# The first expert of the first pair of blocks is summed without gates and multiplied later; the flag of the general path is read four supersteps on

## The chip, the cores and the metric

The kernel runs on one core of one Trainium2 chip. The metric is the device time of one execution in microseconds (us). The engines are TensorE (PE; its weight loads are listed as PEld), VectorE (DVE), ScalarE (ACT), GpSimd (POOL) and SyncE (SP), which here only issues transfers.

## The reference, cut to what matters

A gated linear attention over 4 x 768 tokens, a squared-ReLU layer (384 to 2048 to 384), and then a mixture of eight experts, in which each of the 3072 tokens goes through every expert and the gates P weight the sums:

```python
logits = x @ w_gate
P = np.exp(logits - logits.max())
for _ in range(8):
    P /= P.sum(1, keepdims=True) + 1e-09
    P /= P.sum(0, keepdims=True) + 1e-09
    P *= N / E
out = np.zeros((N, D), dtype=np.float32)
for e in range(E):
    h = np.maximum(x @ w1[e], 0.0)
    ye = h @ w2[e]
    out += P[:, e:e + 1] * ye
```

P needs the logits of all tokens and eight rounds of sums over rows and columns (the Sinkhorn iterations). The expert sums `ye` need no gates until they are weighted.

## The kernel before

Two stages follow one another. The first computes attention and the squared-ReLU layer and writes x2, the input of the experts, to DRAM; it ends at about 594 us. The second is the mixture. It works through three pairs of blocks of 512 tokens; for each pair, through the eight experts; for each expert, through four steps of 256 hidden units. Every matmul of an fp32 product is done three times, on high and low parts.

A **step** runs eight products (`product`, L678; 33 matmuls of 512 columns) named `p1`, `p2`, `p6`, `p5`, `p3`, `p7`, `p22`, `p4`, in this order on PE. They share banks of PSUM, so DVE and ACT have to take sums out between them: ACT copies `s` (L696), DVE forms `t` (`part`, L700) and four sums `v` (`whole`, L705; `whole b` is the first). `p22` writes the bank that `part` reads. ACT makes the high part of the hidden values (L713), DVE the low part (L718). The weights of a step come through `rawa` and `rawc`: POOL forms sums (L650 to L652), ACT high parts (L663), DVE low parts, here called residuals (L667).

Two steps make a **superstep** `q`, of which there are 48, two to an expert and pair. It ends with six tiles `o` (`second`, L729; 12 matmuls each, 2 token blocks `t` by 3 output blocks `m`), which have two PSUM banks. DVE evicts each (`weigh`, L744): it multiplies the tile by the gates `pb` of its tokens, which a transfer has broadcast over the partitions (`ldp`, L736), into the accumulator `acc` for an expert's first superstep of a pair and otherwise into a scratch tile `sc`, which POOL adds to `acc` (`gather`, L749). After the last expert SP stores `acc`.

The gates are made while the first superstep runs: per iteration DVE's row part (L960 to L964), a column sum on PE (`csum`, L967, two passes) and DVE's column part (L971 to L974); then PE transposes P (`pt`, L845), ACT copies it (`pts`, L850), SP stores it (`ptd`, L853) and loads it as `pb`.

A **flag** tells whether the decays of the attention were in range. DVE and POOL reduce it (`in_range`, L883 to L886) after superstep 10, and every engine reads it into a register (L887); at the end a branch on it runs a general path, or not.

The order of all of this on each engine is planned ahead. `Plan` holds steps with an engine, a duration, a due time and needs. `order` plays them through a model of engines that take the step with the earliest due time among the ready ones, and `emit` writes the program in that order. A step that is given other needs can so move on every engine. On the chip each engine takes its instructions in the order written.

```python
add(("skr", it), "dve", 1.7, d, lambda: sk.rows(P), [done], lag=0.8)
add(("skt", it), "pe", 0.1, d, csum, [("skr", it)])
add(("skc", it), "dve", 0.9, d, sk_cols, [("skt", it)])
```

Of the kernel before, what the change touches and what calls it, by code (L numbers as in the profile page):

```python
# [9 lines left out]
F32 = mybir.dt.float32  # L10
# [26 lines left out]
TB = 512  # L37
# [113 lines left out]
def body(tc, fkq, v, wm, wa, wc, gate, seqs, out):  # L151
# [585 lines left out]

    def weigh(q, t, m):
        p, e, s = pair_of(q)
        if e == 0 and s == 0:  # L740
            dst = acc[p, t, m] = pools["acc"].tile([128, TB], F32, name=f"acc{t}{m}")
        else:
            dst = sc[q, t, m] = pools["v"].tile([128, TB], F32, tag="sc", name="sc", bufs=2)
        dve.tensor_tensor(out=dst, in0=ob[q, t, m], in1=pbt[p, e][:, t * TB:(t + 1) * TB], op=ALU.mult)  # L744

    def gather(q, t, m):
        p, e, s = pair_of(q)
        if e or s:
            pool.tensor_tensor(out=acc[p, t, m], in0=acc[p, t, m], in1=sc[q, t, m], op=ALU.add)  # L749
        if e == NE - 1 and s == NST // 2 - 1:  # L750
            o = (2 * p + t) * TB
            sp.dma_start(out=out[m, :, o:o + TB], in_=acc[p, t, m])
# [29 lines left out]
    for g in range(NSTEP):  # L782
        p, r = divmod(g, NE * NST)
        u = at(t_step(g))
        uw = u - 6.0
        plan.load(("ldwa", g), 393, uw - 1.5, lambda g=g: ldwa(g), slot_of["wa", g])
        plan.load(("ldwc", g), 393, uw - 1.4, lambda g=g: ldwc(g), slot_of["wc", g])
        add(("wsum", g), "pool", 1.7, uw, lambda g=g: w_sum(g), [("ldwa", g)])
        for k in "abc":

            n = 3 * g + "abc".index(k) - NWP
            if n >= 0:
                free = ("p4", n // 3) if n % 3 < 2 else ("o", n // 6, 1, 2)
            else:
                free = ("e2", n1 - NF + n + NWP)
            add(("w2hi", g, k), "act", 0.6 if k == "b" else 0.82, uw, lambda g=g, k=k: w2_hi(g, k),
                [("ldwc", g) if k == "c" else ("ldwa", g), ("wsum", g) if k == "b" else None, free,
                 ("w2hi", g, "abc"["abc".index(k) - 1]) if k != "a" else ("w2hi", g - 1, "c") if g else None])
            add(("w2lo", g, k), "dve", 0.7 if k == "b" else 0.96, uw, lambda g=g, k=k: w2_lo(g, k), [("w2hi", g, k)])
        needs = {"p1": [("w2lo", g, "a"), ("w2lo", g, "b"), ("take", g - 1, 3)], "p2": [("whole", g - 1, "b")], "p6": [("take", g, 1)],  # L800
                 "p5": [("whole", g - 1, "c"), "right"], "p3": [("whole", g - 1, "d")], "p7": [("take", g, 2)], "p22": [("part", g)],
                 "p4": [("whole", g - 1, "e")]}
        if r == 0:
            needs["p1"] += [("xlo", p, n) for n in range(3)]
        for n, name in enumerate(PROD):
            if g == 0:
                needs[name] = [d for d in needs[name] if not (isinstance(d, tuple) and d[1] == -1)]
            add((name, g), "pe", 0.68 * len(PROD[name][1]), u + 0.1 * n, lambda g=g, name=name: product(g, name), needs[name] + [last_pe])
            last_pe = (name, g)
        for n, name in ((1, "p1"), (2, "p6"), (3, "p7")):  # L810
            old = {1: "b", 2: "d", 3: "e"}[n]
            add(("take", g, n), "act", 0.6, u + 0.3, lambda g=g, n=n: take(g, n), [(name, g), ("whole", g - 1, old) if g else None])
        add(("part", g), "dve", 0.69, u + 0.3, lambda g=g: part(g), [("p5", g), ("take", g, 2), "right", ("whole", g - 1, "d") if g else None])
        order = "bdce"
        for k, src, other in (("b", "p2", ("take", g, 1)), ("d", "p3", ("part", g)), ("c", "p22", ("take", g, 3)), ("e", "p4", ("take", g, 3))):
            add(("whole", g, k), "dve", 0.69, u + 0.5, lambda g=g, k=k: whole(g, k), [(src, g), other, "right"] + [("whole", g, order[order.index(k) - 1]) if k != "b" else ("whole", g - 1, "e") if g else None]
                + [("hlo", g, "b") if k == "e" else ("hlo", g - 1, order[order.index(k) + 1]) if g else None])
            t, f = TF[k]
            add(("hhi", g, k), "act", 0.61, u + 0.6, lambda g=g, k=k: hid_hi(g, k),
                [("whole", g, k), ("o", g // 2 - 1, t, 2) if g >= 2 else None])  # L820
            add(("hlo", g, k), "dve", 0.69, u + 0.6, lambda g=g, k=k: hid_lo(g, k), [("hhi", g, k)])
        if g % 2 == 0:
            continue
        q = g // 2
        p, e, s = pair_of(q)
        if s == 0:
            n = p * NE + e
            old = pair_of(q - 2 * (NST // 2)) if n >= 2 else None
            plan.load(("ldp", p, e), 524, u - 3.0, lambda p=p, e=e: ldp(p, e), ["P", "right", ("ev", q - NST // 2 - 1, 1, 2) if n >= 2 else None])
        for t in range(2):  # L830
            for m in range(KD):
                d = at((q + 1) * T_SUP - T_E2) + 0.9 * (KD * t + m)
                i = KD * t + m
                free = ("ev", q, (i - 2) // KD, (i - 2) % KD) if i >= 2 else (("ev", q - 1, (i + 4) // KD, (i + 4) % KD) if q else None)
                add(("o", q, t, m), "pe", 2.72, d, lambda q=q, t=t, m=m: second(q, t, m),
                    [("hlo", 2 * q + f // 2, k) for f in range(4) for k in TF if TF[k] == (t, f % 2)] + [("w2lo", 2 * q, "c"), ("w2lo", 2 * q + 1, "c"), free, last_pe])
                last_pe = ("o", q, t, m)
                add(("ev", q, t, m), "dve", 0.69, d + 0.9, lambda q=q, t=t, m=m: weigh(q, t, m), [("o", q, t, m), ("ldp", p, e), ("ac", q - 1, t, m) if q else None,
                     ("ac", q, (i - 2) // KD, (i - 2) % KD) if i >= 2 else ("ac", q - 1, (i + 4) // KD, (i + 4) % KD) if q else None])
                add(("ac", q, t, m), "pool", 1.35, d + 0.9, lambda q=q, t=t, m=m: gather(q, t, m), [("ev", q, t, m)])  # L840

    def gates_turn(n):
        tmp["pt"] = ps_m.tile([24, 4, 128], F32, tag="m", name="pt")
# [38 lines left out]
    def in_range():  # L882
        dve.tensor_reduce(out=mx, in_=minf, axis=AX.XY, op=ALU.min)  # L883
        dve.tensor_scalar(out=mx, in0=mx, scalar1=MIN_DECAY, scalar2=None, op0=ALU.is_lt)
        pool.partition_all_reduce(gmx, mx, 128, bass.bass_isa.ReduceOp.max)
        dve.tensor_copy(out=flag, in_=gmx)  # L886
        general.append(nc.values_load(flag[0:1, 0:1], min_val=0, max_val=1))  # L887

    add("range", "dve", 1.0, n1 + 200, in_range, ["P", ("o", 10, 1, 2)])

    with tc.manual_schedule():
        plan.emit(keep_warm)
# [277 lines left out]
```

## Time and profile before

| | us |
|---|---|
| median of 3 runs | 2159.89 (2159.45 to 2163.94) |
| the profiled execution | 2158.78, of which its span 2157.1 |
| PE busy | 2083.4, 97% of the span |
| DVE, ACT, POOL busy | 1323.9, 886.1, 646.8 |

The profile is one execution. Its timeline gives start, length, engine, line, operation and tile of each group of neighbouring instructions, and in brackets how long the engine was idle before it and what ended that. Instructions of one engine overlap by some hundredths of a microsecond in it. [...]

### The profile page before, as it was taken

What the parts mean: (1) busy time and instruction counts of PE and PEld (TensorE: products, weight loads), DVE (VectorE), ACT (ScalarE), POOL (GpSimd) and SP (SyncE); (2) the same over time, 40 slices, a digit from 0 to 9 for tenths busy, and PEclk for the clock granted to TensorE, in tenths of its full rate; (3) what the DMA queues carried; (4) which work ended last, traced back from release to release, by engine and by line L of the source; (5) the groups of instructions that cost most, each with busy time, mean ns of one, the idle gap of its engine ahead of it and who ended that gap; (6) DMA issues with size and microseconds to landing.
All of it is one profiled execution on the core that took longest, in us unless ns stands there. A gap on an engine that the chain in (4) does not pass through costs nothing.

```text
span 2157.1 us, 27848 instructions
## 1 busy us (share of the span) xinstructions
PE 2083.4 (97%) x10686; PEld 1765.9 (82%) x10686; DVE 1323.9 (61%) x2016; ACT 886.1 (41%) x1505; POOL 646.8 (30%) x642
## 2 busy tenths in 40 slices
PE   7889999999959999999999999999999999999998
PEld 5779899999947888887887888888887888888886
DVE  8973444332465676675677666667668666766663
ACT  4754444444623343343344334334434433433341
POOL 4531101100102334333423333333333233343332
PEclk9899999999979999999999999999999999999999
DMA  7331222110201111121123121112113111211210
GB/s 265 126 126 64 76 82 73 54 44 7 85 34 53 59 60 62 56 69 47 52 73 108 54 69 54 62 52 69 55 54 127 55 55 58 65 57 54 69 45 31
DMA packets 55114, 148.76 MB, mean 69 GB/s; under 512 B 6332, under 2 KB 15548, under 8 KB 54972
## 3 DMA queue, kind: packets, MB, share of 16 engines
q1 hardware_dynamic: 54972, 146.90, 20.7%
q8 instruction: 85, 1.39, 0.3%
q14 instruction: 57, 0.47, 0.1%
HBM read 135.28 MB, written 9.54 MB: 67 GB/s over the span
## 4 chain that ended last, share of the span: by engine, by line
PE 89%; DVE 6%; DMA 1%; issue 1%; POOL 1%; ACT 1%; SPq 0%; POOLq 0%; DVEq 0%; ACTq 0%
PE o L729 35%; PE e L678 33%; PE a L525 8%; PE e L499 8%; PE y L383 1%; PE y L386 1%; PE pp L344 1%; DVE cv_t L923 1%; PE lg L540 1%; DVE cv_t L915 1%; DVE lo L515 1%; DVE sg L318 1%; DVE cv_t L919 0%; POOL acc L749 0%; PE ds L366 0%
## 5 line engine op out<-in xcount | busy, mean ns | idle before, releaser
L729 PE MATMUL o<-h,w 128*128 128x512 f32 x3456 | 794.6, 390 | 7.4 <-DVE acc L744 7.4
L729 PEld LDWEIGHTS o<-h,w 128*128 128x128 f32 x3456 | 650.4, 188 | 143.7 <-DVE acc L744 7.9
L678 PE MATMUL e<-x,w 128*128 128x512 f32 x3168 | 732.8, 391 | 9.7 <-DVE flag L886 4.6
L678 PEld LDWEIGHTS e<-x,w 128*128 128x128 f32 x3168 | 597.7, 189 | 136.2 <-ACT s L696 5.6
L749 POOL TENSOR_TENSOR acc<-acc,sc 128x512 f32<-128x512 f32 x270 | 350.0, 1303 | 574.0 <-DVE sc L744 565.7
L696 ACT COPY s<-e 128x512 f32<-128x512 f32 x288 | 169.1, 587 | 849.6 <-PE e L678 844.8
L744 DVE TENSOR_TENSOR sc<-o,pb 128x512 f32<-128x512 f32 x270 | 186.3, 690 | 384.6 <-PE o L729 349.4
L718 DVE SCALAR_TENSOR_TENSOR h<-v,h 128x512 fp32r<-128x512 f32 x384 | 276.7, 740 | 1.7 <-ACT h L713 1.3
L713 ACT ACTIVATE h<-v 128x512 fp32r<-128x512 f32 x384 | 242.5, 632 | 41.8 <-DVE v L705 41.8
L650 POOL TENSOR_TENSOR rawa<-rawa 128x256 f32<-128x256 f32 x96 | 83.4, 869 | 550.2 <-DMA rawa<-in_wa_dram 375.8
L705 DVE TENSOR_TENSOR v<-e,s 128x512 f32<-128x512 f32 x288 | 198.2, 688 | 75.2 <-ACT w L663 58.1
L499 PE MATMUL e<-x,w 128*128 128x384 f32 x1152 | 228.0, 341 | 10.9 <-DVE w L283 7.4
L499 PEld LDWEIGHTS e<-x,w 128*128 128x128 f32 x1152 | 199.8, 189 | 17.7 <-DVE w L283 8.8
L515 DVE TENSOR_TENSOR lo<-g,hi 128x384 fp32r<-128x384 f32 x128 | 85.0, 666 | 206.3 <-ACT hi L511 206.3
L525 PE MATMUL a<-hi,w 128*128 128x384 f32 x768 | 199.5, 341 | 0.0
L667 DVE TENSOR_TENSOR w<-rawa,w 128x768 fp32r<-128x768 f32 x192 | 158.0, 824 | 7.4 <-ACT w L663 7.4
L663 ACT CAST w<-rawa 128x768 fp32r<-128x768 f32 x192 | 135.2, 729 | 27.9 <-POOL rawa L652 9.3
L525 PE MATMUL a<-lo,w 128*128 128x384 f32 x384 | 131.0, 341 | 11.0 <-DVE lo L515 10.9
L525 PEld LDWEIGHTS a<-hi,w 128*128 128x128 f32 x768 | 139.9, 191 | 1.5 <-issue 0.3
L504 ACT ACTIVATE g<-e 128x384 f32<-128x384 f32 x128 | 62.9, 491 | 178.0 <-PE e L499 157.3
L328 POOL TENSOR_TENSOR kq<-kq,sg 128x512 f32<-128x512 f32 x24 | 30.9, 1287 | 289.4 <-DVE sg L318 172.1
L667 DVE TENSOR_TENSOR w<-rawc,w 128x768 fp32r<-128x768 f32 x96 | 91.6, 954 | 0.3 <-ACT w L663 0.2
(99 smaller groups left out, 1300.8 us busy)
## 6 DMA issues: line engine op xcount, KB each, us to landing
rawa<-in_wa_dram SPq DMA_DIRECT2D x96, 384.0 KB, 3.0
rawc<-in_wc_dram SPq DMA_DIRECT2D x96, 384.0 KB, 3.4
raw<-in_wm_dram SPq DMA_DIRECT2D x16, 768.0 KB, 6.1
pb<-ptd SPq DMA_DIRECT2D x24, 512.0 KB, 3.6
fraw<-in_fkq_dram SPq DMA_DIRECT2D x23, 512.0 KB, 3.8
kq<-in_fkq_dram SPq DMA_DIRECT2D x23, 512.0 KB, 4.4
vt<-in_v_dram SPq DMA_DIRECT2D x24, 192.0 KB, 4.9
x2d<-x2t SPq DMA_DIRECT2D x8, 576.0 KB, 2.8
```

The source lines that it names most:

```text
L499: pe.matmul(ps, w[:, wl, k * 128:(k + 1) * 128], xx[:, xl, k, :], start=n == 0, stop=n == 3 * KD - 1)
L525: pe.matmul(acc1[j][m], w[:, wl, D + m * 128:D + (m + 1) * 128], g, start=f == 0 and n == 0, stop=f == NF - 1 and n == 2)
L663: act.copy(out=W2[g, k][:, 0, 0:n], in_=src)
L667: dve.tensor_tensor(out=W2[g, k][:, 1, 0:n], in0=src, in1=W2[g, k][:, 0, 0:n].bitcast(F32), op=ALU.subtract)
L678: pe.matmul(ps, w[a], x[b], start=start and n == 0, stop=stop and n == 2, skip_group_check=True)
L696: act.copy(out=snap[g, n], in_=bank[g, "a"])
L705: dve.tensor_tensor(out=vs[g, k], in0=bank[g, k], in1=other, op=ALU.add)
L713: act.activation(out=hs[g // 2, t, f][:, 0], in_=vs[g, k], func=ACTF.Relu)
L718: dve.scalar_tensor_tensor(out=h[:, 1], in0=vs[g, k], scalar=0.0, in1=h[:, 0].bitcast(F32), op0=ALU.max, op1=ALU.subtract)
L729: pe.matmul(ob[q, t, m], w[:, a, c:c + 128], h[:, b], start=f == 0 and n == 0, stop=f == 3 and n == 2)
L744: dve.tensor_tensor(out=dst, in0=ob[q, t, m], in1=pbt[p, e][:, t * TB:(t + 1) * TB], op=ALU.mult)
L749: pool.tensor_tensor(out=acc[p, t, m], in0=acc[p, t, m], in1=sc[q, t, m], op=ALU.add)
```

## The change

For expert 0 of the first pair (supersteps 0 and 1) `weigh` uses no gates: superstep 0's tiles are copied into `acc`, superstep 1's are added to it by DVE. After that POOL multiplies each `acc` by the gates once (`scale0`), in place, and superstep 2's additions to it wait for this. The evictions of these two supersteps no longer need `ldp`. In the very last superstep DVE, not POOL, does the additions of `gather`. The reduction of the flag stays after superstep 10, its read (`choose`) waits for superstep 14.

```diff
     def weigh(q, t, m):
         p, e, s = pair_of(q)
+        if p == 0 and e == 0:
+
+            if s == 0:
+                acc[p, t, m] = pools["acc"].tile([128, TB], F32, name=f"acc{t}{m}")
+                dve.tensor_copy(out=acc[p, t, m], in_=ob[q, t, m])
+            else:
+                dve.tensor_tensor(out=acc[p, t, m], in0=ob[q, t, m], in1=acc[p, t, m], op=ALU.add)
+            return
...
+    def scale0(t, m):
+        pool.tensor_tensor(out=acc[0, t, m], in0=acc[0, t, m], in1=pbt[0, 0][:, t * TB:(t + 1) * TB], op=ALU.mult)
+
     def gather(q, t, m):
         p, e, s = pair_of(q)
+        eng = dve if q == NSUP - 1 else pool
         if e or s:
-            pool.tensor_tensor(out=acc[p, t, m], in0=acc[p, t, m], in1=sc[q, t, m], op=ALU.add)
+            eng.tensor_tensor(out=acc[p, t, m], in0=acc[p, t, m], in1=sc[q, t, m], op=ALU.add)
...
-                add(("ev", q, t, m), "dve", 0.69, d + 0.9, lambda q=q, t=t, m=m: weigh(q, t, m), [("o", q, t, m), ("ldp", p, e), ("ac", q - 1, t, m) if q else None,
+                add(("ev", q, t, m), "dve", 0.69, d + 0.9, lambda q=q, t=t, m=m: weigh(q, t, m), [("o", q, t, m), ("ldp", p, e) if p or e else None, ("ac", q - 1, t, m) if q else None,
...
-                add(("ac", q, t, m), "pool", 1.35, d + 0.9, lambda q=q, t=t, m=m: gather(q, t, m), [("ev", q, t, m)])
+                if p == 0 and e == 0:
+                    add(("ac", q, t, m), "none", 0, d + 0.9, lambda: None, [("ev", q, t, m)])
+                    if s == NST // 2 - 1:
+                        add(("sc0", t, m), "pool", 1.35, d + 1.5, lambda t=t, m=m: scale0(t, m), [("ac", q, t, m), ("ldp", 0, 0)])
+                else:
+                    last = q == NSUP - 1
+                    add(("ac", q, t, m), "dve" if last else "pool", 0.69 if last else 1.35, d + 0.9, lambda q=q, t=t, m=m: gather(q, t, m),
+                        [("ev", q, t, m), ("sc0", t, m) if p == 0 and e == 1 and s == 0 else None])
...
+
+    def choose():
         general.append(nc.values_load(flag[0:1, 0:1], min_val=0, max_val=1))
 
     add("range", "dve", 1.0, n1 + 200, in_range, ["P", ("o", 10, 1, 2)])
+    add("choose", "dve", 0.1, n1 + 230, choose, ["range", ("o", 14, 1, 2)])
```

How the change moves instructions is seen at three places. In these rows a number behind a name (`e_5852`) tells one buffer from another, `x7` is a count, and brackets name the engines or transfers that are waited for.

The first place is PE at the gates. Before, the seven remaining column sums and the transpositions stand between the second and the third `o` tile of superstep 0:

```order
L729 MATMUL o<-h,w_5072 128x512 x6
L729 MATMUL o<-h,w_5260 128x512 x6
L967 MATMUL csum<-sk_cs,sk_ones 128x8 [waits DVE_49] x7
L845 MATMUL pt<-shift,P 24x128 [waits DVE_49]
L845 MATMUL pt<-shift,P 24x128 x3
L845 MATMUL pt<-shift,P 24x128 [waits Activation_49]
L845 MATMUL pt<-shift,P 24x128 x3
L729 MATMUL o<-h,w_5072 128x512 [waits DVE_49]
```

Now the sums are spread over the tiles of superstep 0 and the two steps of superstep 1; this is the end of the second step, up to the first `o` of superstep 1:

```order
L678 MATMUL e_5828<-x_5132,w_5583 128x512 x2
L989 MATMUL csum<-sk_cs,sk_ones 128x8 [waits DVE_49] x2
L678 MATMUL e_5852<-x_5131,w_5406 128x512 [waits DVE_49]
L678 MATMUL e_5852<-x_5131,w_5406 128x512 x2
L678 MATMUL e_5906<-x_5131,w_5583 128x512 x3
L678 MATMUL e_5906<-x_5131,w_5406 128x512 x3
L864 MATMUL pt<-shift,P 24x128 [waits DVE_49]
L864 MATMUL pt<-shift,P 24x128 x3
L864 MATMUL pt<-shift,P 24x128 [waits Activation_49]
L864 MATMUL pt<-shift,P 24x128 x3
L729 MATMUL o<-h,w_5354 128x512 x6
```

Here the last two sums are neighbours, `e_5852` with three matmuls is `p22`, the two rows of `e_5906` are `p4`, and the transpositions stand ahead of superstep 1's tiles instead of superstep 0's third.

The second place is DVE at the gates. Before, the iterations follow one another there, and the first evictions come behind the last column part:

```order
L964 TENSOR_REDUCE sk_cs<-P 128x8 [waits DVE_49]
L971 TENSOR_SCALAR sk_cs<-csum 128x8 [waits PE_49]
L972 RECIPROCAL sk_cs<-sk_cs 128x8 [waits DVE_49]
L973 TENSOR_SCALAR sk_cs<-sk_cs 128x8 [waits DVE_49]
L974 TENSOR_TENSOR P<-P,sk_cs 128x192 [waits DVE_49]
L744 TENSOR_TENSOR acc_5749<-o,pb 128x512 [waits DMAHW4_49]
L744 TENSOR_TENSOR acc_5751<-o,pb 128x512
```

Now steps of superstep 1 stand between the iterations; these rows are what lies on DVE behind the column sum that is the last but one:

```order
L718 SCALAR_TENSOR_TENSOR h<-v,h 128x512 [waits Activation_49] x2
L993 TENSOR_SCALAR sk_cs<-csum 128x8 [waits PE_49]
L994 RECIPROCAL sk_cs<-sk_cs 128x8 [waits DVE_49]
L995 TENSOR_SCALAR sk_cs<-sk_cs 128x8 [waits DVE_49]
L996 TENSOR_TENSOR P<-P,sk_cs 128x192 [waits DVE_49]
L982 TENSOR_REDUCE sk_rs<-P 128x24 [waits DVE_49]
L983 TENSOR_SCALAR sk_rs<-sk_rs 128x24 [waits DVE_49]
L984 RECIPROCAL sk_rs<-sk_rs 128x24 [waits DVE_49]
L985 TENSOR_TENSOR P<-P,sk_rs 128x192 [waits DVE_49]
L986 TENSOR_REDUCE sk_cs<-P 128x8 [waits DVE_49]
L718 SCALAR_TENSOR_TENSOR h<-v,h 128x512 [waits Activation_49]
L700 TENSOR_TENSOR t<-e_5852,s_5860 128x512
```

The last column sum on PE takes the `sk_cs` of the third row from below, and the `p22` behind it takes the bank that the last row (`part`) reads.

The third place is DVE at the flag, before:

```order
L883 TENSOR_REDUCE mx<-minf 128x1
L884 TENSOR_SCALAR mx<-mx 128x1 [waits DVE_49]
L886 CAST flag<-gmx 128x1 [waits Pool_49]
L887 TENSOR_LOAD flag [waits DVE_49]
L705 TENSOR_TENSOR v<-e_8426,s_8433 128x512 [waits PE_49,Activation_49]
L667 TENSOR_TENSOR w_8454<-rawa,w_8454 128x768 [waits DMAHW1_49,Activation_49]
L700 TENSOR_TENSOR t<-e_8463,s_8467 128x512 [waits PE_49,Activation_49]
```

and now:

```order
L902 TENSOR_REDUCE mx<-minf 128x1
L903 TENSOR_SCALAR mx<-mx 128x1 [waits DVE_49]
L905 CAST flag<-gmx 128x1 [waits Pool_49]
L705 TENSOR_TENSOR v<-e_8420,s_8427 128x512 [waits PE_49,Activation_49]
L667 TENSOR_TENSOR w_8434<-rawa,w_8434 128x768 [waits DMAHW1_49,Activation_49]
L700 TENSOR_TENSOR t<-e_8443,s_8447 128x512 [waits PE_49,Activation_49]
```

The read (`TENSOR_LOAD`) has gone from there, on PE, ACT, POOL and SP as well, to the beginning of superstep 15; the cast, which waits for POOL, is still ahead of `whole b`, a residual and `part`.

## Rows read from the trace of the kernel before

**Rows 1.** The page: the chain by engine, and the group of evictions (busy, mean ns)

```profile
PE 89%; DVE 6%; DMA 1%; issue 1%; POOL 1%; ACT 1%; SPq 0%; POOLq 0%; DVEq 0%; ACTq 0%
...
L744 DVE TENSOR_TENSOR sc<-o,pb 128x512 f32<-128x512 f32 x270 | 186.3, 690 | 384.6 <-PE o L729 349.4
```

**Rows 2.** PE's waits: in total (us), times, longest

```profile
PE csum L967 <- DVE sk_cs L964: 18.1, 6, 3.1
```

**Rows 3.** The timeline of PE around the gates (start, length, engine, line)

```profile
616.61 0.28 PE L967 MATMUL csum<-sk_cs,sk_ones 128*128 128x8 f32 x2
620.04 0.39 PE L967 MATMUL csum<-sk_cs,sk_ones 128*128 128x8 f32 x2 [3.15 <-DVE sk_cs L964]
...
641.16 1.03 PE L845 MATMUL pt<-shift,P 128*24 128x128 f32 x4 [0.66 <-ACT pts L850]
649.60 13.67 PE L729 MATMUL o<-h,w 128*128 128x512 f32 x48 [7.41 <-DVE acc L744]
663.11 15.12 PE L678 MATMUL e<-x,w 128*128 128x512 f32 x66
678.07 12.18 PE L729 MATMUL o<-h,w 128*128 128x512 f32 x53
```

**Rows 4.** The chain that ended last, in order of time: start, us, what

```profile
642.83 1.99 DMA ptd<-pts
644.88 3.95 DMA pb<-ptd
...
678.23 16.32 PE o L729 x72
```

**Rows 5.** The timeline at the flag, DVE and PE

```profile
975.91 2.20 PE L678 MATMUL e<-x,w 128*128 128x512 f32 x9
...
982.01 0.15 DVE L886 CAST flag<-gmx 128x1 int32<-128x1 f32 x1 [4.89 <-POOL gmx L885]
...
982.76 14.86 PE L678 MATMUL e<-x,w 128*128 128x512 f32 x57 [4.65 <-DVE flag L886]
983.28 0.69 DVE L705 TENSOR_TENSOR v<-e,s 128x512 f32<-128x512 f32 x1 [1.11 <-issue]
983.89 0.95 DVE L667 TENSOR_TENSOR w<-rawa,w 128x768 fp32r<-128x768 f32 x1
```

**Rows 6.** The timeline of DVE: one Sinkhorn iteration, ends of its two parts

```profile
635.89 0.35 DVE L960 TENSOR_REDUCE sk_rs<-P 128x24 f32<-128x192 f32 x1
...
637.22 0.50 DVE L964 TENSOR_REDUCE sk_cs<-P 128x8 f32<-128x192 f32 x1
...
638.40 0.17 DVE L971 TENSOR_SCALAR sk_cs<-csum 128x8 f32<-128x8 f32 x1 [0.69 <-PE csum L967]
...
639.05 0.36 DVE L974 TENSOR_TENSOR P<-P,sk_cs 128x192 f32<-128x192 f32 x1
```

**Rows 7.** Windows of PE: us, PE busy (count), granted clock, DMA share, GB/s

```profile
620.00:622.00 2.00, 0.39 (x2) 0.71 0.05 18
...
654.00:656.00 2.00, 2.00 (x8) 0.76 0.00 0
...
982.00:983.00 1.00, 0.24 (x1) 0.82 0.00 0
...
986.00:987.00 1.00, 1.00 (x6) 0.97 0.00 0
...
1140.00:1142.00 2.00, 1.40 (x7) 1.00 0.02 8
1142.00:1144.00 2.00, 0.69 (x3) 1.00 0.26 97
```

**Rows 8.** The timeline of DVE and POOL: a residual at 615, and the tail

```profile
615.66 0.68 DVE L667 TENSOR_TENSOR w<-rawa,w 128x512 fp32r<-128x512 f32 x1
...
2147.53 0.69 DVE L744 TENSOR_TENSOR sc<-o,pb 128x512 f32<-128x512 f32 x1 [2.03 <-PEq L894]
2148.30 1.26 POOL L749 TENSOR_TENSOR acc<-acc,sc 128x512 f32<-128x512 f32 x1 [1.43 <-DVE sc L744]
```

More of the change, by code (lines that the diff above doesn't have):

```diff
@@ L828, in body @@
             old = pair_of(q - 2 * (NST // 2)) if n >= 2 else None
-            plan.load(("ldp", p, e), 524, u - 3.0, lambda p=p, e=e: ldp(p, e), ["P", "right", ("ev", q - NST // 2 - 1, 1, 2) if n >= 2 else None])
+            plan.load(("ldp", p, e), 524, u - 3.0, lambda p=p, e=e: ldp(p, e), ["P", "right", ("ev", q - NST // 2 - 1, 1, 2) if n >= 2 else None, ("sc0", 1, 2) if n == 2 else None])
         for t in range(2):
```

## The prediction

> **What bounds the kernel now.** I read the chain that ended last first: 89% of it is TensorE (PE) [rows 1]. So only stretches in which PE stands or runs at its lower clock are worth anything. PE's waits name the largest, the column sums of the gates [rows 2]; PE's own timeline shows what lies around it [rows 3]. Between 616.61, where 24 `o` matmuls are through, and 649.60 us PE runs seven column sums and the transpositions of the gates, nothing else. In order, that is: the Sinkhorn iterations on VectorE (DVE), two transpositions, the store of the gates, the broadcast load `pb`, and the first eviction that multiplies by `pb`; PE has only two `o` banks, and both are full. A second stretch is the read of the flag, a third the tail after the last matmul.
>
> **Prices.** A 512-column matmul at full clock: 16.32 / 72 = 0.227 us [rows 4], so an `o` tile of twelve is 2.72 us. A 128x512 DVE step takes 0.61 us to the start of the next (983.28 to 983.89), a 768-column one 0.95 - 0.08 = 0.87 [rows 5]. A Sinkhorn iteration on DVE: its rows 635.89 to 637.72, 1.83 us; its columns 638.40 to 639.41, 1.01; together 2.84 [rows 6].
>
> **Part 1: the gates leave the path of the first expert.** Removed: the first `o` evictions no longer wait for `pb`. Six multiplications become copies and six become additions on DVE. No row shows a 128x512 copy out of PSUM on DVE; I take the 0.69 us of the multiplication that it replaces [rows 1], and between 0.35 and 0.75 nothing changes below, since the copies wait for PE. POOL loses six additions of `q` = 1 and gets six multiplications of the same shape: nothing.
>
> The new order interleaves the seven remaining column sums with the matmuls, so both engines have to be walked. Nothing differs up to 616.61. From there PE has four `o` tiles (10.88), the nine matmuls `p1` and `p2` of the next step (2.04) and two column sums (0.15 each, an estimate from the 0.28 of two passes [rows 3]): it is through with `p2` at 629.9. DVE keeps up that far: six copies, two weight residuals and two iterations are 6 x 0.61 + 1.5 + 2 x 2.84 = 10.8 of these 13.3 us, and each copy comes right behind its tile.
>
> From 629.9 DVE is the bound. Up to the step `part` (L700) of the second step, for which PE's `p22` waits, its order holds four iterations (11.36) and ten 128x512 steps (6.1): 17.5 us, so `part` ends at 647.4. PE has less to do and stands four times: about 0.7 us before the first `p22`, 0.3 before the sixth of the seven sums, and then 3.9 us between two neighbouring column sums, because a whole iteration and two DVE steps lie between them; and 0.9 more for `part`. After 647.4 PE has nine matmuls, the two groups of transpositions (2 x 1.03 and 0.66 between them at the lower clock [rows 3]), and then the `o` tiles of the second superstep, which started at 678.07 before.
>
> The clock decides the last step. After PE stopped at 616.9, with a column sum at 620.04, the granted clock left 1.0 at about 620.8 (0.71 over 620 to 622), and it was back at about 655.0, after 5.4 us of matmuls; at the flag it fell at 982.6 after a stop at 978.1 and was back at 986.06, after 3.3 us [rows 7]. The stop from 642.5 to 647.4, with one column sum in it, is like these. So I take half clock (1.2 GHz) for the nine matmuls and the transpositions: 647.4 + 4.1 + 2.7 = 654.2. Gain: 678.07 - 654.2 = **23.9 us**. If the clock holds, nine matmuls take 2.04, and ScalarE's chain (L713, then `pts`) makes the second transposition end at about 652: gain 26. If every one of the four iterations shows a hop of 0.4 to PE and back, the gain is 22.3. PE's own work, with no wait and no fall, would end at about 644.5: 33.6 is the most that is there.
>
> What is late next: gates are ready at about 654, `pb` lands 2 + 4 us later [rows 4] at about 660, and its first reader is now POOL (`scale0`), ahead of the weight sums of step 6. These reach PE at about 701. Four multiplications of 1.3 us have some 30 us of slack. The loads of step 5 stand between `ptd` and `pb` in SP's queue and are needed at about 678; they land by 660.
>
> **Part 2: the flag.** Only the read moves. DVE still runs the cast of the flag, which waits for POOL's reduction, until 982.16 [rows 5]: DVE stays blocked from 977.1, with whatever stands behind it. Before, PE stood behind its own read: superstep 11's 66 matmuls took from 975.91 to 997.46 (982.76 + 14.86, less the 0.16 by which neighbouring groups overlap in this view: 663.11 + 15.12 against 678.07 [rows 3]), 21.55 us against 66 x 0.227 = 14.96: 6.6 lost, 4.65 standing and the rest at the lower clock. Now PE goes on after `p2` until `p22`, 24 matmuls after 975.91, at 981.35. `p22` needs `part`, and DVE reaches it after the cast, `whole b` and a weight residual: 982.16 + 0.61 + 0.87 + 0.69 = 984.3. PE stands 3.0 us instead. Gain **3.6 us** if the clock holds, 3.6 - 1.65 = 1.95 if it falls (half of the 3.3 us). A stop of 1.91 (0.60 and 1.31 in two windows) left it at 1.00 [rows 7]; those of 3.15 and more did not. 3.0 lies nearer to the second, but the fall after 616.9 came only in the following stop; I take no fall.
>
> The read itself stands four supersteps on, when the flag is long there. From the end of the cast to PE's next matmul were 0.60 us [rows 5], so its price is 0 to 0.6; DVE and ScalarE have it in idle time (DVE's `whole b` waits for PE there). [...] No row here shows a read with its flag ready. [...] I take **0.2** of the 0 to 0.6, nearer to the hidden end, since nine matmuls (2.04 us) stand before the read.
>
> **Part 3: the last superstep's additions go to DVE.** The last eviction ends at 2148.22 and POOL's addition at 2149.56 [rows 8]. A DVE step of this shape with SBUF operands takes 0.68 (615.66) and follows after 0.61: it ends at 2148.82. Gain **0.7 us** (0.5 to 0.8). The other five fit between evictions, which are 2.7 us apart.
>
> **Sum.** 23.9 + 3.6 - 0.2 + 0.7 = 28.0 us. The profiled execution took 2158.78 us (span 2157.1 and 1.7 around it); that gives 2130.8. The median of the runs shown, 2159.89, lies 1.1 above it; I forecast against it: 2131.9, said as **2131.5**.
>
> **Rivals.** (a) *The column sums hold PE's queue.* PE takes instructions in order, so a sum whose DVE half is late holds the matmuls behind it. In my walk only one does so for long. If the five sums placed among `e` matmuls each cost what a sum cost before (18.1 / 6 = 3.0 us [rows 2]), less the 4.2 counted, part 1 loses 10.8: 2142. For it: DVE is full from 630 on. Against: the iterations have `e` steps between them that PE needs anyway, so waits overlap. 15%. (b) *The flag's stall only changes its name*: DVE blocked as long, PE at `p22` with the clock fallen and 0.6 for the read: 2131.5 + 2.1 = 2133.6, or, with no gain at all, 2135.5. That the change does nothing there is contained in this. 20%. (c) *More*: the clock holds at 647 and falls nowhere: 2131.5 - 2.1 = 2129.4, down to 2127 with shorter iterations at full clock. 15%. (d) *Slower*: POOL's `scale0` waits for `pb` in front of the weight sums. It costs PE from the point at which `pb` lands later than about 690, 30 us after my 660, and makes the kernel slower than before only past 718. Since the load was 4 us [rows 4] and the gates' chain has no other wait, 2%. My forecast, 2129.5 to 2134: 48%.
>
> **How the numbers follow.** 80% lie between 2127 and 2139: forecast, (b), (c) and the near half of (a), with the bounds 22.3 to 26 of part 1, 0 to 5.4 of the flag and 0 to 0.6 of the read in it. Within 0.2% of the time before, about what a measurement of this kernel can tell from no change, would need a loss of 24 us of the gain: 1%. Faster 97%, slower 2%.
>
> **What would show it.** Right: `o` tiles run through from 611 to about 628, PE's longest stop there is one of about 4 us between two neighbouring column sums near 642, the second superstep's `o` tiles start near 654; at the flag (about 24 us earlier) PE stands about 3 us before a `p22` on DVE, and nothing on the read; the last step is a DVE addition 0.6 us after the last eviction. Wrong: several stops of 3 us on `sk_cs` among the `e` matmuls (a), a POOL release of PE through the weights (d), or a stop at `p22` of 4 us and more followed by granted 0.5 (b).

## The result and the profile after

The changed kernel takes **2132.03 us** (median; 2130.82 to 2134.19) against 2159.67 us of the kernel before run beside it: a ratio of 0.987, 95% interval 0.9857 to 0.9883. Run again later beside the experiments, it took 2131.05 (2129.93 to 2132.11), a ratio of 0.9874 (0.9859 to 0.9889). The forecast was 2131.5. The gain is 27.6 us, and 27.8 in the second comparison; the sum had 28.0.

The waits of PE in the changed kernel, in us in total, times, longest. The 18.1 us on column sums [rows 2] are one wait of 3.6; the read of the flag is gone from the list, and the waits for `t` (`part`) have grown from 0.8 us to 5.3. Before and then now:

```profile
PE e L678 <- DVE flag L886: 4.6, 1, 4.6
...
PE e L678 <- DVE t L700: 0.8, 1, 0.8
```

```profile
PE e L678 <- DVE t L700: 5.3, 5, 2.7
...
PE csum L989 <- DVE sk_cs L986: 3.6, 1, 3.6
```

PE's timeline at the gates in the changed kernel, which answers to [rows 3] (start, us, what; idle time before it in brackets):

```profile
609.02 0.28 PE L989 MATMUL csum<-sk_cs,sk_ones 128*128 128x8 f32 x2
609.16 8.45 PE L729 MATMUL o<-h,w 128*128 128x512 f32 x36
...
632.59 0.96 PE L678 MATMUL e<-x,w 128*128 128x512 f32 x3 [0.58 <-DVE t L700]
...
640.97 0.39 PE L989 MATMUL csum<-sk_cs,sk_ones 128*128 128x8 f32 x2
644.94 0.39 PE L989 MATMUL csum<-sk_cs,sk_ones 128*128 128x8 f32 x2 [3.58 <-DVE sk_cs L986]
646.14 4.21 PE L678 MATMUL e<-x,w 128*128 128x512 f32 x9 [0.81 <-DVE t L700]
650.15 1.06 PE L864 MATMUL pt<-shift,P 128*24 128x128 f32 x4
651.87 0.72 PE L864 MATMUL pt<-shift,P 128*24 128x128 f32 x4 [0.66 <-ACT pts L869]
652.35 16.89 PE L729 MATMUL o<-h,w 128*128 128x512 f32 x72
669.07 15.12 PE L678 MATMUL e<-x,w 128*128 128x512 f32 x66
```

The `o` tiles now run on from the first sum, the seven others are spread over the next 36 us, and one stop of 3.58 us between two neighbouring sums is left. The windows of PE there (us, PE busy, and the granted clock, the share of TensorE's full clock that it was given): the clock stays at 1.00 through the stop and falls in the window in which PE takes up work again.

```profile
642.00:644.00 2.00, 0.00 (x0) 1.00 0.00 0
644.00:646.00 2.00, 0.39 (x2) 0.83 0.00 0
646.00:652.00 6.00, 5.19 (x14) 0.50 0.00 0
652.00:654.00 2.00, 2.00 (x11) 0.96 0.03 8
```

The flag in the changed kernel, a timeline of all engines, which answers to [rows 5]:

```profile
950.59 5.60 PE L678 MATMUL e<-x,w 128*128 128x512 f32 x24
...
956.16 0.38 POOL L904 PARTITION_ALL_REDUCE gmx<-mx  x1 [5.96 <-issue]
956.57 0.15 DVE L905 CAST flag<-gmx 128x1 int32<-128x1 f32 x1 [4.76 <-POOL gmx L904]
...
958.86 9.38 PE L678 MATMUL e<-x,w 128*128 128x512 f32 x33 [2.67 <-DVE t L700]
...
963.30 1.29 POOL L761 TENSOR_TENSOR acc<-acc,sc 128x512 f32<-128x512 f32 x1 [6.76 <-issue]
963.34 1.81 DVE L718 SCALAR_TENSOR_TENSOR h<-v,h 128x512 fp32r<-128x512 f32 x1
...
968.69 2.35 PE L678 MATMUL e<-x,w 128*128 128x512 f32 x9 [0.45 <-DVE t L700]
```

PE passes its old stop and stands for `part` instead, 2.67 us. Behind that come two things that [rows 5] do not show: POOL comes back only 6.76 us after its reduction, and DVE's step beside it takes 1.81 us instead of 0.68.

**Places.** Four stretches, each from one PE milestone to the next, separate what the change did from what varies by chance. *First sum*: the start of the column sum ahead of superstep 0's `o` tiles, before which no instruction differs. *Gates*: from there to the first product of superstep 2. *Superstep 2* and *superstep 11*: from the first product to that of the next superstep; 31.28 us if PE never stops. The stretches are of the one execution of each kernel that was profiled; the gain is that of the medians, against the kernel before run beside each (us). The intervals of the ratios are 2 to 4 us wide to either side in most rows, so gains that lie closer together are told apart by the stretches alone.

| kernel | first sum | gates | superstep 2 | superstep 11 | median | gain |
|---|---|---|---|---|---|---|
| before | 610.93 | 83.46 | 31.28 | 37.96 | 2159.67 | |
| changed | 609.02 | 60.05 | 31.28 | 36.66 | 2132.03 | 27.6 |
| changed, again | 609.34 | 58.90 | 31.28 | 35.39 | 2131.05 | 27.8 |
| gates only | 609.46 | 59.86 | 31.28 | 38.71 | 2134.48 | 24.1 |
| flag only | 610.33 | 83.15 | 31.28 | 35.72 | 2156.29 | 2.3 |
| cast late | 612.99 | 59.66 | 31.28 | 37.56 | 2134.81 | 23.8 |
| stops filled | 610.41 | 57.83 | 31.28 | 36.02 | 2131.31 | 27.3 |
| flag on TensorE | 610.27 | 59.11 | 31.27 | 31.55 | 2126.51 | 32.3 |
| iterations spread | 610.43 | 49.89 | 34.47 | 36.35 | 2124.97 | 33.8 |
| both of these | 609.21 | 49.86 | 34.59 | 31.55 | 2120.89 | 37.9 |
| gates closer | 610.60 | 60.47 | 36.27 | 31.55 | 2131.95 | 27.2 |
| scaling late | 611.06 | 59.68 | 32.26 | 36.27 | 2133.91 | 26.8 |

The span of the changed kernel's profiled execution is 2130.4 us, 26.7 under the span before: 1.9 of it ahead of the first sum, where nothing was changed; 23.4 at the gates; 1.3 in superstep 11; 0.9 at the end; and 0.8 lost at the two changes of pair, where PE waits for ScalarE's `s` (4.3 us in all before, 5.1 now). The first sum stands anywhere from 609.0 to 613.0 in these twelve traces. So of two profiled executions only the stretches can be compared.

### The profile page after: what moved, and what is told of

It is laid out like the page before. It is cut to its first block, busy times and chain, and to the rows that moved or that the text cites. A ratio compares the mean times of both kernels' runs of the same rounds, so it can differ in the third digit from the quotient of the medians.

```text
span 2130.4 us, 27837 instructions
## 1 busy us (share of the span) xinstructions
PE 2080.0 (98%) x10686; PEld 1762.8 (83%) x10686; DVE 1325.2 (62%) x2022; ACT 886.4 (42%) x1505; POOL 638.1 (30%) x636
## 4 chain that ended last, share of the span: by engine, by line
PE 90%; DVE 6%; issue 1%; DMA 1%; POOL 1%; ACT 0%; SPq 0%; DVEq 0%; POOLq 0%; ACTq 0%
PE o L729 35%; PE e L678 33%; PE e L499 9%; PE a L525 8%; PE y L383 1%; PE y L386 1%; PE pp L344 1%; DVE cv_t L937 1%; DVE cv_t L945 1%; PE lg L540 1%; DVE lo L515 1%; PE ds L366 0%; DVE cv_t L941 0%; DVE w L283 0%; DVE sg L318 0%
## 5 line engine op out<-in xcount | busy, mean ns | idle before, releaser
L761 POOL TENSOR_TENSOR acc<-acc,sc 128x512 f32<-128x512 f32 x258 | 334.4, 1303 | 536.4 <-DVE sc L752 529.5
L752 DVE TENSOR_TENSOR sc<-o,pb 128x512 f32<-128x512 f32 x264 | 182.0, 690 | 372.3 <-PE o L729 339.1
```

What stands on the lines that cost most here:

```text
L761: eng.tensor_tensor(out=acc[p, t, m], in0=acc[p, t, m], in1=sc[q, t, m], op=ALU.add)
```

## The experiments

**The two halves.** The gates alone, without the moved read and with the last additions left on POOL; and the moved read alone:

```diff
 gates only (against the changed kernel)
-        eng = dve if q == NSUP - 1 else pool
+        eng = pool
...
-    def choose():
...
-    add("choose", "dve", 0.1, n1 + 230, choose, ["range", ("o", 14, 1, 2)])
```

```diff
 flag only (against the kernel before)
+    def choose():
         general.append(nc.values_load(flag[0:1, 0:1], min_val=0, max_val=1))
...
+    add("choose", "dve", 0.1, n1 + 230, choose, ["range", ("o", 14, 1, 2)])
```

> Only part 1 of the change: the first expert of the first pair is summed without gates; the flag is read where it was before, and POOL does the last superstep's additions. My theory (part 1 is nearly all of it, 23.4 us by the trace of the changed kernel: 23.8 up to the second superstep's o tiles, less 0.4 of lower clock in them): 2159.7 - 23.4 = 2136.3, that is 4.3 slower than the changed kernel if the parts add up as predicted (3.6 - 0.2 + 0.7), and 2.0 slower if the flag is worth only the 1.3 that the trace shows. At the flag PE stands 4.6 us on the read again and takes 21.5 us for superstep 11's 66 matmuls; around the gates its rows are those of the changed kernel (one stop of 3.6, one of 0.8). Rival (the 1.9 us by which the profiled execution was ahead before the first changed instruction belongs to the change): the column sum ahead of the first o tile stands at 609.0 here too; by my theory it varies from execution to execution with nothing changed.

> Only the later read of the flag, all else as before. By my prediction's step (PE stands 3.0 us on DVE and the clock holds): 3.4 faster than before, 2156.3. By the trace of the changed kernel (PE stands 2.7 us at the first p22, the clock falls, DVE's steps are slowed afterwards and PE stands 0.45 more): 1.3 faster, 2158.4, with superstep 11's 66 matmuls in 20.3 us against 21.5. [...]

Measured: 2134.48 us, ratio 0.9886 (0.9871 to 0.9901), and 2156.29, ratio 0.9985 (0.9976 to 0.9994). The gates give 24.1 us, the flag 2.3. The first is part 1's 23.9; against the changed kernel 2.4 to 3.4 us are missing, where 4.3 or 2.0 were expected. The second is a real gain, between the two that were expected (3.4 and 1.3), and less than the 3.6 of part 2. What the changed kernel has beyond both, 27.6 - 24.1 - 2.3 = 1.2, holds the tail and the spread of medians.

**What the flag's stop consists of.** Two kernels attack it from two sides. In the first, the cast of the flag moves from the reduction to the read, so that DVE never waits for POOL in superstep 11:

```diff
         pool.partition_all_reduce(gmx, mx, 128, bass.bass_isa.ReduceOp.max)
-        dve.tensor_copy(out=flag, in_=gmx)
 
     def choose():
+        dve.tensor_copy(out=flag, in_=gmx)
         general.append(nc.values_load(flag[0:1, 0:1], min_val=0, max_val=1))
```

> The changed kernel with the cast of the flag, which waits for POOL's reduction, moved behind superstep 14 as well, ahead of the read. My theory (DVE, blocked 4.8 us by the cast, is what is left at the flag): PE stands nowhere in superstep 11, the granted clock stays at 1.00, its 66 matmuls take 15.0 to 15.5 us against 20.3: 5 us faster than the changed kernel, 2127. Rival 1 (POOL's own absence, 6 us before and 7 us behind its reduction, delays the weights or DVE by other ways): 66 matmuls in 16 to 20 us with a stop on weights or on DVE steps slowed by POOL; 2128 to 2132. Rival 2 (the stop moves to superstep 14, since the cast has a wait there too): no gain, a stop behind superstep 14.

Measured: 2134.81 us, ratio 0.988 (0.9865 to 0.9895); superstep 11 takes 37.56 us, no better than 36.66. PE no longer stops for `part`: all 66 products run through. The stop has moved to the `o` tiles, and behind it the clock is at 0.50 in the windows from 974 to 978. The expected 2127 us were missed; the stop has the cause of the first rival, at a time above the rival's 2128 to 2132. The timeline of this kernel there:

```profile
967.60 1.72 POOL L761 TENSOR_TENSOR acc<-acc,sc 128x512 f32<-128x512 f32 x1 [7.58 <-DVE v L705]
...
971.12 0.62 ACT L663 CAST w<-rawa 128x512 fp32r<-128x512 f32 x1 [5.17 <-POOL rawa L652]
971.64 0.62 ACT L713 ACTIVATE h<-v 128x512 fp32r<-128x512 f32 x1
...
972.32 0.50 PE L729 MATMUL o<-h,w 128*128 128x512 f32 x1 [1.67 <-ACT h L713]
...
974.12 16.19 PE L729 MATMUL o<-h,w 128*128 128x512 f32 x58 [1.30 <-DVE h L718]
```

POOL's next addition starts 7.6 us after the reduction, the weight sums of the next step come behind it, ScalarE's cast of those weights waits 5.17 us, and the hidden values queued behind that cast are what PE waits for. That DVE stands behind the cast is therefore one of two ways in which the same absence of POOL reaches PE.

In the second, 29 products that nobody reads fill PE's three long stops: 15 between the neighbouring sums, 3 behind them, 11 before `p22` at the flag. Shown is the part at the flag and the function:

```diff
+        if (g, name) == (22, "p22"):
+            fill(11, 22)
...
+    def fill(n, g):
+        t = pools["o"].tile([128, TB], F32, tag="o", name="fill")
+        for _ in range(n):
+            pe.matmul(t, wop(g, "b11")[0], xop(0, "a11")[0], start=True, stop=True)
```

> The changed kernel with 29 more matmuls whose results nobody reads, in PE's stops: 15 between the two neighbouring column sums and 3 behind them, 11 ahead of the p22 at the flag (0.227 us each). If the stops cost through the clock as well: it stays at 1.00 at both places; at the gates the nine matmuls take 2.05 us against 4.2 and the transpositions with the wait between them less, the second superstep's o tiles start about 1.5 to 2.5 us earlier counted from the first column sum; at the flag superstep 11's 66 matmuls take 18.5 us against 20.3. Together 3 to 4 faster than the changed kernel: 2128.5. Rival (the time is lost to DVE's order, and the clock's part is hidden by DVE or ScalarE, which are no faster): within 0.7 of the changed kernel.

Measured: 2131.31 us (2128.55 to 2132.68), ratio 0.9867 (0.9852 to 0.9882), which can't be told from the changed kernel: the 3 to 4 us that were expected did not come. The stretches show what each place gave. PE's timeline:

```profile
642.40 0.39 PE L1003 MATMUL csum<-sk_cs,sk_ones 128*128 128x8 f32 x2
642.64 3.71 PE L883 MATMUL fill<-x,w 128*128 128x512 f32 x15
646.40 0.39 PE L1003 MATMUL csum<-sk_cs,sk_ones 128*128 128x8 f32 x2
```

The second sum stands exactly as far behind the first as without the products (4.00 us against 3.97): DVE sets this distance, PE only waits. With PE busy, the clock stays at 1.00 in every window from 640 to 658, and the gates take 57.83 us against 60.05 and 58.90 (58.90 to 60.05 in the six executions with the changed kernel's gates). So the half clock of part 1 costs 1.1 to 2.2 us, for which the sum had 2.1. At the flag the clock stays at 1.00 as well, in the windows from 955 to 963, and superstep 11 still takes 36.02: the clock is not what keeps it from 31.3.

**The cause at the flag.** If POOL's absence is the cause, the reduction has to leave POOL. One product of TensorE with the matrix of ones that the column sums use counts the partitions with the flag set; the minimum with 1 makes it a flag again:

```diff
-        pool.partition_all_reduce(gmx, mx, 128, bass.bass_isa.ReduceOp.max)
-        dve.tensor_copy(out=flag, in_=gmx)
+    def range_sum():
+        tmp["r"] = ps_m.tile([128, 1], F32, tag="m", name="rsum")
+        pe.matmul(tmp["r"], sk.ones, mx, start=True, stop=True)
+    def range_flag():
+        dve.tensor_scalar(out=gmx, in0=tmp["r"], scalar1=1.0, scalar2=None, op0=ALU.min)
+        dve.tensor_copy(out=flag, in_=gmx)
...
```

> The changed kernel with the flag's reduction over partitions made by TensorE (one product of a 128x1 column with the ones of the Sinkhorn sums, then min with 1 and the cast on DVE) instead of PARTITION_ALL_REDUCE on POOL; the read stays four supersteps on. Theory: what is left of the stop in superstep 11 comes from POOL alone, which is away for about 6 us before and 7 us behind the reduction, so that the cast of the flag, the next weights and the sums come late. Then superstep 11, from its first product to that of superstep 12, takes 31.3 to 31.9 us instead of 36.66, the granted clock stays at 1.00 there, and the time is 2126.7 (2125 to 2129). Rival: the stop comes from DVE's order in this superstep or from where the flag's steps stand, and stays: superstep 11 at 35 or more, time 2131 to 2133.

Measured: 2126.51 us (2125.67 to 2127.94), ratio 0.9853 (0.984 to 0.9866). PE's timeline of this superstep, whole:

```profile
950.89 15.12 PE L678 MATMUL e<-x,w 128*128 128x512 f32 x66
965.86 0.28 PE L907 MATMUL rsum<-mx,sk_ones 128*128 128x1 f32 x2
965.99 16.61 PE L729 MATMUL o<-h,w 128*128 128x512 f32 x72
982.44 15.12 PE L678 MATMUL e<-x,w 128*128 128x512 f32 x66
```

31.55 us and no stop; the clock stays at 1.00 in the windows from 950 to 970, and the two other kernels with this reduction give 31.55 as well. Of the 4.1 to 5.4 us that superstep 11 loses in the changed kernel 0.3 are left: the rest came from one reduction on POOL. Before the change 6.7 were lost, of which the moved read took away the smaller part. The new reduction with the read at its old place was not run.

**The changed kernel again**, to see what varies by itself:

> The changed kernel once more, beside the others on the same chip: 2132 (2130 to 2134.5). In its trace the first csum ahead of superstep 0's o tiles stands anywhere from 609 to 613 us, as in the five traces so far, superstep 1's o tiles start 43.3 us behind it, superstep 11 takes 36.7 us; if the flag's stop is one of chance, superstep 11 differs by over 1 us.

Measured: 2131.05 us. Two stretches differ from what was expected. Superstep 1's `o` tiles start 42.3 us behind the first sum, not 43.3: behind the stop between the neighbouring sums the clock is back at 1.00 from 650, in the first execution only from 653 (0.93 in the window before). PE's timeline of the second execution:

```profile
609.34 0.28 PE L989 MATMUL csum<-sk_cs,sk_ones 128*128 128x8 f32 x2
...
651.62 16.79 PE L729 MATMUL o<-h,w 128*128 128x512 f32 x72
```

And superstep 11 takes 35.39 instead of 36.66, so its stop is partly one of chance. There PE's stop before `p22` is the same (2.68 us against 2.67), but the clock does not fall. The windows of the first execution and then of this one (us; busy time of PE, PEld, DVE, ACT and POOL; granted clock):

```profile
958.00:959.00 1.00, 0.14 (x1) 0.14 (x2) 1.00 (x3) 1.00 (x3) 0.00 (x0) 1.00 0.00 0
959.00:960.00 1.00, 1.00 (x4) 0.75 (x5) 1.00 (x3) 0.22 (x1) 0.00 (x0) 0.67 0.02 8
960.00:961.00 1.00, 1.00 (x4) 0.81 (x3) 1.00 (x3) 0.63 (x1) 0.00 (x0) 0.50 0.00 0
```

```profile
958.00:959.00 1.00, 0.95 (x4) 0.82 (x5) 1.00 (x2) 0.40 (x1) 0.00 (x0) 1.00 0.00 0
959.00:960.00 1.00, 1.00 (x6) 0.79 (x5) 1.00 (x3) 0.63 (x1) 0.00 (x0) 1.00 0.03 8
```

Of the five executions profiled with this stop (these two, the flag alone, the spread iterations, the late scaling), the clock fell behind it in four; in that with the late scaling this is read from the 9.26 us of the 33 matmuls behind the stop, which took 7.80 where the clock held and 9.38 in the first execution.

**The bound at the gates.** Part 1 says that DVE is the bound from 629.9 because iterations crowd into one stretch of products. With the gates off the path they can go elsewhere: three of the iterations are tied to `o` tiles of superstep 1, the last to the first product of superstep 2. A second kernel has this and the reduction on TensorE:

```diff
+        after = {4: ("o", 1, 0, 0), 5: ("o", 1, 0, 2), 6: ("o", 1, 1, 1), 7: ("p1", 4)}
-        add(("skr", it), "dve", 1.7, d, lambda: sk.rows(P), [done], lag=0.8)
+        add(("skr", it), "dve", 1.7, d, lambda: sk.rows(P), [done, after.get(it)], lag=0.8)
```

> The changed kernel with Sinkhorn iterations 4 to 6 tied to the o tiles of superstep 1 and iteration 7 to the first product of superstep 2 (one more dependence each, same arithmetic), so that four fewer iterations stand among superstep 1's products. Theory: from 629.9 us on DVE is the bound because five iterations stand in one stretch of products, and with the gates off the path they can be spread freely: the products of superstep 1 take 15 to 16.5 us instead of 26.2, the iterations among the o tiles cost PE two short sums each, iteration 7 and the two transpositions cost 0.5 to 2 us in superstep 2. The clock does not fall. Time 2123 (2121 to 2125.5). Rival: the iterations cost as much where they go (PE stops of 2 to 4 us before csum among the o tiles, or superstep 3 waits for the gates that now come 30 us later): time 2129 or more.

> Both edits, the reduction on TensorE and the spread iterations. If both theories hold the gains add: 5.3 and 9 off 2132, so 2118 (2116 to 2121). If one of them only moves its stop, 2123 to 2128.

Measured: 2124.97 us, ratio 0.9844 (0.9831 to 0.9858), and 2120.89 (2120.63 to 2123.79), ratio 0.983 (0.9816 to 0.9843), the fastest of all. The gain of spreading is 33.8 - 27.8 = 6.0, not 9; the two gains add, 4.5 and 6.0 alone and 10.1 together. The gates' stretch gave what was expected (49.89 against 58.90), and superstep 2 took 3.2 back. The timelines of the first of the two, PE, POOL and DVE:

```profile
629.71 13.21 PE L678 MATMUL e<-x,w 128*128 128x512 f32 x57
...
660.18 0.28 PE L990 MATMUL csum<-sk_cs,sk_ones 128*128 128x8 f32 x2
...
675.89 9.60 POOL L755 TENSOR_TENSOR acc<-acc,pb 128x512 f32<-128x512 f32 x6 [20.91 <-DMA pb<-ptd]
...
681.07 2.04 DVE L667 TENSOR_TENSOR w<-rawa,w 128x768 fp32r<-128x768 f32 x1
683.03 1.28 DVE L752 TENSOR_TENSOR sc<-o,pb 128x512 f32<-128x512 f32 x2
683.76 6.43 PE L729 MATMUL o<-h,w 128*128 128x512 f32 x27 [1.55 <-DVE sc L752]
```

Superstep 1's products run without a stop. But `pb` now lands at 675.9, and POOL's six multiplications run beside DVE's work of superstep 2, whose steps with SBUF operands take up to 2.04 us; the evictions behind them come 1.55 us late.

I took that stop for a late `pb` and, in the kernel with both edits, brought the gates forward, with iterations 4 and 5 back among superstep 1's products:

```diff
-        after = {4: ("o", 1, 0, 0), 5: ("o", 1, 0, 2), 6: ("o", 1, 1, 1), 7: ("p1", 4)}
+        after = {6: ("o", 1, 0, 0), 7: ("o", 1, 0, 2)}
```

> The kernel with both edits (reduction on TensorE, iterations spread), but iterations 4 and 5 free again among superstep 1's products and 6 and 7 tied to its first and third o tile, so that the gates are ready some 10 us earlier. Theory: in the kernel with both edits superstep 2's o tiles stood 1.6 us because its evictions, the first that multiply by the gates of expert 1, waited for a late pb; with gates 10 us earlier this stop goes (1.6 to 1.9 us) and superstep 2's products lose the two transpositions and the sum (1.3), while superstep 1 gets back two sums, a stop of 0.6 and the transpositions (1.5 to 2). From the first csum ahead of the o tiles to the first product of superstep 3: 82.8 us (82 to 83.5) instead of 84.45, time 2119.5 (2118 to 2121). Rival: the stop in superstep 2 has another cause and stays, and the two iterations bring the long stop between neighbouring sums back: 85 us or more, 2121 or more.

Measured: 2131.95 us, ratio 0.9876 (0.986 to 0.9893); the gates and superstep 2 together 96.7 us instead of 84.45. Both numbers of this expectation were missed, by the side on which its rival stood. PE, POOL and DVE:

```profile
653.72 7.33 PE L729 MATMUL o<-h,w 128*128 128x512 f32 x24 [2.59 <-DVE acc L746]
...
675.39 10.04 POOL L755 TENSOR_TENSOR acc<-acc,pb 128x512 f32<-128x512 f32 x6 [11.79 <-DMA pb<-ptd]
...
682.26 2.04 DVE L667 TENSOR_TENSOR w<-rawc,w 128x768 fp32r<-128x768 f32 x1
...
687.23 3.19 PE L678 MATMUL e<-x,w 128*128 128x512 f32 x8 [2.79 <-DVE t L700]
```

DVE enters superstep 1's `o` tiles with a backlog, and an iteration that stands ahead of the first eviction in its order holds both `o` banks; the gates come no earlier at all (`pb` at 675.4), and POOL's multiplications now fall among products, where PE stops 2.79 us for `part`.

**The price of POOL's multiplications alone.** In the changed kernel they run among the `o` tiles of superstep 1 and cost nothing that can be seen. One more dependence puts them beside the products of superstep 2:

```diff
-    [("ac", q, t, m), ("ldp", 0, 0)])
+    [("ac", q, t, m), ("ldp", 0, 0), ("p1", 4)])
```

> The changed kernel with one more dependence: POOL's six multiplications by the first expert's gates wait for the first product of superstep 2, so that they run back to back beside superstep 2's products (about 671 to 680 us) instead of among the o tiles of superstep 1. No wait on pb is added, and the weight sums of step 6, due at about 701, come no later than 690. Theory: the multiplications cost PE through DVE, whose steps with SBUF operands take 1.2 to 2 us instead of 0.68 while POOL runs, as in the two kernels with later gates; in a stretch of products DVE has no slack: superstep 2, from its first product to that of superstep 3, takes 33.5 us (32.5 to 35.5) instead of 31.3, time 2133.5 (2132 to 2136). Rival, which the prediction held: the multiplications have 30 us of slack and cost only through pb or the weight sums: superstep 2 stays at 31.3 to 31.6, time 2130 to 2132.

Measured: 2133.91 us, ratio 0.9875 (0.9859 to 0.9892); superstep 2 takes 32.26 us, between the two expectations (32.5 to 35.5, and 31.3 to 31.6 by the rival). The direction holds; the loss, 1.0 us, is a little under half of the 2.2 expected. A DVE step beside POOL:

```profile
669.45 8.72 POOL L755 TENSOR_TENSOR acc<-acc,pb 128x512 f32<-128x512 f32 x6
...
673.65 1.67 DVE L667 TENSOR_TENSOR w<-rawa,w 128x768 fp32r<-128x768 f32 x1
```

So the slowed DVE alone costs 1.0 us; that superstep 2 lost 3.2, 3.3 and 5.0 in the three kernels with later gates is this together with what else lies there (an iteration and transpositions in the first two, DVE's backlog in the third, and a clock that must have fallen there: the nine matmuls at 687.23 took 3.62 us, those at 643.09 2.37). How much each of those has was not separated.

## Why the prediction was right, and where it was off

**What bounds the kernel**: right. The three stretches named (gates, flag, tail) hold the whole gain that does not vary by chance.

**Part 1, 23.9 us**: right in size and in its steps. The walk put `part` 36.5 us behind the first sum and superstep 1's `o` tiles 43.3 behind it (647.4 and 654.2 less 610.93); they stand 37.1 and 43.3 behind it in the trace. The four stops were 0.7, 0.3, 3.9 and 0.9 in the walk and 0.58, 0.4 (640.97 against 637.85 and 12 products), 3.58 and 0.81 in the trace. The assumed fall of the clock came, where it was assumed, but its length varies: in the second execution it was shorter (back at 1.00 from 650, not 653), and the `o` tiles stood at 42.3. The agreement with 43.3 to the tenth is therefore luck; the walk is right to about 1 us. The gates alone gave 24.1. No run shows the 1.2 GHz of the prediction; of the half clock the windows show a share of 0.50 (646 to 652), at which the nine matmuls took 4.21 us, against 4.1 in the walk. Rival (a), sums that hold PE for 3 us each, is refuted: one does.

**Part 2, 3.6 us**: right in the place and the name of the new stop, too large in size: 2.3 with the flag alone, 1.3 to 2.6 in superstep 11's length in the changed kernel's two executions. The stop before `p22` is what the walk made it: `p22` starts 8.27 us behind the superstep's first product, in the walk 8.4 (984.3 less 975.91). Two steps failed. "I take no fall": it fell in four executions of five; the gain that the sum gives for that, 1.95, is near what was measured. And the walk ended at `part`: POOL, which comes back 6.8 us after its reduction, makes DVE and then PE late once more (0.45 us before the last nine products in the first execution; 0.17, and 0.24 among the `o` tiles, in the second). Rival (b) had the clock; neither had POOL.

**The read, 0.2 us**: it costs nothing. PE's register is loaded 2 us before the first product of superstep 15, while the `o` tiles still run, and the products follow without a gap. First the group of the line, then PE's timeline:

```profile
L908 PEldq TENSOR_LOAD <-flag x1: 487/487/487, 1079.1 to 1079.1; - x1
```

```profile
1081.09 3.11 PE L678 MATMUL e<-x,w 128*128 128x512 f32 x13
```

The 0.2 in the sum was the author's estimate within 0 to 0.6; no run shows a read that costs it, and this one, with its flag ready, cost 0.

**Part 3, 0.7 us**: right. From the start of the last eviction to the end of the last addition are 1.41 us, on DVE, against 2.03 [rows 8]:

```profile
2121.64 0.69 DVE L752 TENSOR_TENSOR sc<-o,pb 128x512 f32<-128x512 f32 x1 [1.30 <-PE o L729]
2122.36 0.69 DVE L761 TENSOR_TENSOR acc<-acc,sc 128x512 f32<-128x512 f32 x1
```

**The sum**: 28.0 against 27.6 measured. 24.1 + 2.3 + 0.6 = 27.0 by the terms as measured. Part 1 was 0.2 low and part 2 1.3 high, which the width of the medians nearly hides: that the total came out to half a microsecond is in part luck. The step from 2131.9 to 2131.5 is given no reason in the prediction.

**Rival (d)** had the wrong mechanism for its price. It let POOL's multiplications cost nothing until the weight sums were late, some 30 us on. They cost 1.0 us as soon as they stand beside products, through DVE. In the changed kernel they don't, so the forecast was not touched by it.

## What to carry to other kernels

When a wait is moved behind other work, look for its source: the read of the flag was only the place where POOL's absence became visible, and the kernels with the read or the cast elsewhere stopped somewhere else, while a product with ones instead of the reduction removed the stop (superstep 11 took 31.55 us). Work that has left the critical path has to be spread over stretches in which its engine is idle, since a planner that starts it as early as it can will crowd it; and an engine that is off the path can still slow one that is on it, as POOL's multiplications did through DVE (1.0 us in superstep 2 with the late scaling). To compare two profiled executions, cut them at milestones with nothing changed ahead of the first.

## What the runs showed of the hardware

- In the changed kernel's first execution the granted clock fell after PE had resumed: at the flag it was still 1.00 in the window in which PE resumed, at 958.86, then 0.67 and 0.50 in the next two. Behind the same stop of 2.7 us it held at 1.00 in the second execution.
- In the changed kernel POOL did nothing for 5.96 us before a PARTITION_ALL_REDUCE of 0.38 us and for 6.76 after it (5.97 and 6.72 in the second execution), with no wait in the profile for either ("issue"); of the 5.96, 4.35 lie behind the end of DVE's step that writes its input. What POOL does in that time no run here tells.
- DVE's steps with both operands in SBUF (`h`, `w`) took mostly 1.2 to 2.0 us instead of 0.68 to 0.95 while POOL ran; those that read PSUM (`v`, `t`) kept their 0.68. Beside POOL's multiplications `h` and `w` took 1.67, 1.18 and 1.18 with the late scaling and up to 2.04 with the iterations spread or the gates closer; `v` and `t` took 0.68 to 0.69 there. Beside POOL's addition at 963.30 in the changed kernel, and the weight sum behind it, `h` took 1.81.
